# Clustered attention with two gated layers: another fetch offset in the planner, w_in in blocks of two half-height pieces with a common scale

## The chip, the cores and the metric

The kernel runs on one core of a Trainium2 chip. The metric is the device time of one execution in microseconds (us); lower is better. The engines are TensorE (PE, with its weight loads as PEld), VectorE (DVE), ScalarE (ACT), GpSimd (POOL) and SyncE (SP, whose queue issues every DMA here). The kernel before took 785.26 us (median of 3 runs, 783.64 to 786.57).

## The reference, cut to what matters

Inputs are q, k and v of 2 batches, 8 heads, 768 positions and 64 channels, 16 centroids for each head, and two weight pairs: w_in of 512x2048 and w_out of 2048x512, drawn as float64.

```python
q_assign = argmax(einsum(q_n, c_n)); k_assign = argmax(einsum(k_n, c_n))
mask   = q_assign[..., :, None] == k_assign[..., None, :]
scores = where(mask, scale * q @ k.T, -1e9)
attn   = exp(scores - max) / (sum + 1e-9)
x  = (attn @ v) as 1536 x 512                                  # both batches
h  = x @ w1_in;  x2  = (h * sigmoid(h)) @ w1_out               # layer 1
h  = x2 @ w2_in; out = (max(h,0) + alpha * min(h,0)) @ w2_out  # layer 2
```

## The kernel before

All operands of a matmul are split into a high and a low fp16 part under a power-of-two scale, so that a product takes three matmuls (high by high, high by low, low by high).

**Attention.** There are 12 query tiles of 128 rows and 8 heads, so 96 units. `front(u)` makes the scores of a unit in two PSUM banks (L793, L797), takes their bound on DVE (L807), the exponential on ACT (L812), the fp16 parts on ACT (L819) and DVE (L821); a DMA transpose (L827) turns them, and `back(u)` multiplies them with v (L839, 18 matmuls) two units later. When the eight heads of a tile are through, `x_done` scales the tile (L865), splits it on POOL (L868, L869) and transposes it (L870). Keys, values and queries are prepared by `prep_k_*`, `prep_v*` and `prep_q_*`, with transposes of their own (L638, L684, L730, L746).

**Weights.** A float64 weight piece arrives as pairs of 32-bit words in a raw buffer of 8 KB for each partition (`load_piece`, L893), 1 MB at a time. `to_f32` makes float32 of it: two ACT passes (L904, L908) and two DVE passes (L915, L918). Then the sum of squares is taken: for the first layer on PE (`sum_sq_pe`, L953, with a DVE reduction at L955), for the second on ACT (L945). For w_in, `scale(j)` sums over the partitions on PE (`all_sum`, L498), makes a power-of-two scale and its inverse (`pow2_scale`: L445 on DVE, L450 and L453 on POOL), splits the piece into its fp16 parts (`split`, mode "a": L930 on ACT, L931 on DVE) and then loads the next piece into the raw buffer that came free. w_in has 8 pieces, each of 256 columns and all 512 rows. The first layer has 4 raw buffers, the second 3, and each layer's w_out follows in the same buffers. w_out's 8 pieces share one scale: all are converted first (`conv`), `scale` sums over them, and only then are they split (`piece`, L930 and L931 again).

**Layers.** Layer 1 runs beside attention in 7 chunks of one or two tiles (`layer1`, L1187 for w1_in and L1218 for w1_out, with a tanh, three elementwise passes at L1194 to L1199 and an ACT copy at L1225). Layer 2 runs in 3 blocks of 512 rows: 16 column tiles through w2_in (L1289, 192 matmuls a block; L1298, L1299, L1302, L1303 on DVE and ACT), then 4 row tiles through w2_out (L1320, 192 matmuls). The second layer's raw buffers and the split parts of w2_in lie where the keys, values and queries of attention lay; those of w2_out where the first layer's weights lay.

**Order.** The program is written in Python in some order, and then `plan_order` fixes the order on every engine. `Plan` holds a cost for each instruction (`costs`), follows the data's dependences, and lays the program out in its own time, 61 times with some noise, forward and backward; the best layout's order is what the engines execute. Two parts of the model matter here. A DMA from DRAM costs a fixed part and its bytes by a rate that depends on the length of a contiguous run (L104 to L106). And PE's instructions are taken to be fetched in blocks of 256: a counter `fetched` starts at some value, is raised by 2 for each matmul (the weight load and the matmul), and when it passes 256 the DMAs in flight at that moment are made later by 0.4 or 1.1 us (L224, L277 to L289). The order is fixed, not the times: an engine waits in its place for whatever is late.

## Time and profile before

| | |
|---|---|
| median of 3 runs | 785.26 us |
| profiled execution | 784.7 us, span 782.8 us |
| PE busy | 679.5 us, 87% of the span |
| DVE, ACT, POOL busy | 541.3, 466.5, 136.2 us |
| DMA packets of the instruction queue | 52, 0.85 MB in all |
| w_in, w_out loads | 16 each, 1024 KB each |
| DMA transposes | 149 |

"Busy" is the time in which an engine executed; a share of the span is an average over stages that differ. The program has five: a start in which keys, queries and weights are prepared (to about 40 us), a stage in which the first layer's weights are converted beside the first units of attention (to 120 us), a short one in which layer 1 has begun but the weights are not all done (to 180 us), the long one with attention and layer 1 side by side (to 440 us), and the preparation of the second layer's weights beside the last of layer 1 (to 560 us). After that PE works through layer 2.

### The profile page before, as it was taken

How to read it: one execution, taken by the hardware profiler on the slowest of the kernel's cores; microseconds unless marked ns; L12 is line 12 of the kernel's file. 1: busy time of each engine (PE TensorE's matmuls, PEld its weight loads, DVE VectorE, ACT ScalarE, POOL GpSimd, SP SyncE). 2: the span in 40 equal slices, each digit the busy share in tenths (PEclk: the TensorE clock that was granted, in tenths of full speed). 3: DMA queues.
4: the chain of work that ended last, by engine and by line, in shares of the span. 5: the costliest groups of instructions: out<-in, count | busy, mean ns of one | idle time of the engine just before them, and what ended most of it. 6: DMA issues, size and time to landing. Idle time of an engine off the chain costs nothing.

```text
span 782.8 us, 16346 instructions
## 1 busy us (share of the span) xinstructions
PE 679.5 (87%) x6730; PEld 475.0 (61%) x6730; DVE 541.3 (69%) x992; ACT 466.5 (60%) x757; POOL 136.2 (17%) x237
## 2 busy tenths in 40 slices
PE   0254559679999999998999999888999999999998
PEld 0243448568887878887788898774444444444443
DVE  4689998898779578867876886878970385018700
ACT  6875976777778667756765898997640141012200
POOL 3562131123404732121130001000000000000000
PEclk9999978899999999999999999999999999999999
DMA  7989997989999996996898986452000000000000
GB/s 216 300 201 294 300 214 125 156 168 152 165 160 158 186 162 129 155 167 125 138 142 135 243 225 187 160 172 100 1 15 27 14 1 0 28 28 1 0 28 27
DMA packets 241593, 101.85 MB, mean 130 GB/s; under 512 B 217328, under 2 KB 227568, under 8 KB 241392
## 3 DMA queue, kind: packets, MB, share of 16 engines
q1 hardware_dynamic: 241520, 100.83, 60.4%
q8 instruction: 52, 0.85, 0.4%
q14 instruction: 21, 0.17, 0.1%
HBM read 44.08 MB, written 3.15 MB: 60 GB/s over the span
## 4 chain that ended last, share of the span: by engine, by line
PE 36%; ACT 7%; DMA 5%; DVE 2%; issue 1%; POOL 0%; SPq 0%; ACTq 0%
PE w L1320 11%; PE w L1289 10%; PE m L1320 5%; PE m L1289 5%; DMA arena<-in_moe_w_out_dram 2%; PE w L1218 2%; ACT arena L904 2%; ACT arena L908 2%; ACT arena L945 1%; PE w L1187 1%; DMA arena<-arena 1%; DMA arena<-in_moe_w_in_dram 1%; PE x L839 1%; PE s L793 1%; PE s L797 1%
## 5 line engine op out<-in xcount | busy, mean ns | idle before, releaser
L1218 PE MATMUL w<-arena 128*128 128x256 f16 (+1 forms) x1248 | 150.1, 258 | 3.7 <-ACT arena L1225 1.9
L1187 PE MATMUL w<-arena 128*128 128x256 f16 (+1 forms) x1200 | 142.0, 257 | 3.1 <-DVE arena L1195 1.7
L1218 PEld LDWEIGHTS <-arena 128*128 128x128 f16 x1344 | 113.2, 99 | 22.3 <-issue 5.7
L1187 PEld LDWEIGHTS <-arena 128*128 128x128 f16 x1344 | 111.9, 98 | 23.3 <-issue 8.3
L821 DVE TENSOR_TENSOR arena<-arena 128x768 f16<-128x768 f32 x96 | 96.8, 1009 | 30.4 <-ACT arena L819 30.0
L839 PE MATMUL x<-arena 128*128 128x64 f16 x1728 | 108.6, 198 | 10.1 <-DMA arena<-arena 8.0
L812 ACT ACTIVATE arena<-s,stat 128x768 f32<-128x768 f32 x96 | 85.9, 895 | 38.1 <-DVE s L807 18.4
L807 DVE TENSOR_SCALAR_CACHE_REDUCE s<-s,stat 128x768 f32<-128x768 f32 x96 | 97.6, 1019 | 12.2 <-PE s L797 10.4
L839 PEld LDWEIGHTS <-arena 128*128 128x128 f16 x1728 | 90.6, 102 | 21.2 <-DMA arena<-arena 10.9
L819 ACT ACTIVATE arena<-arena 128x768 f16<-128x768 f32 x96 | 80.3, 837 | 30.2 <-DMA arena<-arena 29.5
L1320 PEld LDWEIGHTS <-arena 128*128 128x128 f16 x576 | 56.4, 98 | 68.0
L1289 PEld LDWEIGHTS <-arena 128*128 128x128 f16 x576 | 55.7, 98 | 68.5 <-issue 2.4
L1289 PE MATMUL w<-arena 128*128 128x512 f16 x384 | 94.1, 379 | 0.0
L1320 PE MATMUL w<-arena 128*128 128x512 f16 x384 | 85.8, 379 | 0.0
L1298 DVE TENSOR_SCALAR arena<-w,stat 128x512 f32<-128x512 f32 x32 | 23.9, 747 | 78.8 <-PE w L1289 78.7
L793 PE MATMUL s<-arena 80*128 80x384 f16 x192 | 68.6, 357 | 9.9 <-ACT arena L812 9.7
L1302 ACT ACTIVATE arena<-arena,stat 128x512 f16<-128x512 f32 x48 | 34.4, 718 | 69.2 <-DVE arena L1299 69.2
L797 PE MATMUL s<-arena 128*128 128x384 f16 x192 | 68.5, 357 | 0.0
L450 POOL TENSOR_SCALAR stat<-stat 128x1 int32<-128x1 int32 x49 | 12.4, 256 | 290.1 <-DVE stat L445 197.1
L915 DVE SCALAR_TENSOR_TENSOR arena<-arena 128x1024 int32<-128x1024 int32 x32 | 41.3, 1290 | 22.2 <-ACT arena L908 22.1
L1289 PE MATMUL m<-arena 128*128 128x512 f16 x192 | 51.3, 379 | 0.1
L931 DVE SCALAR_TENSOR_TENSOR arena<-arena,stat 128x1024 f16<-128x1024 f32 x32 | 41.6, 1306 | 5.0 <-ACT arena L930 5.0
(145 smaller groups left out, 969.2 us busy)
## 6 DMA issues: line engine op xcount, KB each, us to landing
arena<-in_moe_w_in_dram SPq DMA_DIRECT2D x16, 1024.0 KB, 6.3
arena<-in_moe_w_out_dram SPq DMA_DIRECT2D x16, 1024.0 KB, 5.9
arena<-in_k_dram SPq DMA_DIRECT2D x8, 384.0 KB, 5.1
arena<-in_q_dram SPq DMA_DIRECT2D x6, 512.0 KB, 5.2
arena<-in_v_dram SPq DMA_DIRECT2D x8, 384.0 KB, 6.2
out_dram<-arena SPq DMA_DIRECT2D x12, 256.0 KB, 2.0
arena<-arena SPq DMA_TRANSPOSE x149, 4.0
arena<-in_moe_alpha_dram SPq DMA_DIRECT2D x1, 1024.0 KB, 5.3
```

Source lines behind the costliest of these rows:

```text
L793: nc.tensor.matmul(out=sc[:, j, :hs], lhsT=qt2[0:D + C, h], rhs=kt2[0:D + C, h % 2, j * hs:(j + 1) * hs], start=True, stop=False,)
L797: nc.tensor.matmul(out=sc[:, j, :hs], lhsT=qt1[:, h], rhs=kt1[:, h % 2, j * hs:(j + 1) * hs], start=False, stop=True,)
L807: nc.vector.tensor_scalar(sc[:, :, :hs], sc[:, :, :hs], nd_cols[:, H * (n % 2) + h:H * (n % 2) + h + 1], None, op0=ALU.mult, op1=ALU.min, ...
L812: nc.scalar.activation(out=view(o, F32, 2, hs), in_=sc[:, :, :hs], func=ACTF.Exp, scale=-1.0, bias=bias, accum_out=sums[n % 2][:, h:h + 1],)
L819: nc.scalar.activation(out=hl[:, 0], in_=p, func=ACTF.Copy)
L821: en.tensor_tensor(out=hl[:, 1], in0=p, in1=hl[:, 0], op=ALU.subtract)
L839: nc.tensor.matmul(out=x_ps[0][:, h], lhsT=pt[:, ph * T + t], rhs=vt[:, h % 2, t, vh], start=(i == 0), stop=(i == 3 * T - 1),)
L931: nc.vector.scalar_tensor_tensor(out=lo, in0=t, scalar=s, in1=hi, op0=ALU.mult, op1=ALU.subtract)
L1187: nc.tensor.matmul(out=hp[:, ff], lhsT=wi[:, a, kd, ff * 128:ff * 128 + 128], rhs=mov(bb, kd), start=(i == 0), stop=(i == 3 * KD - 1),)
L1218: nc.tensor.matmul(out=acc, lhsT=wo[:, a, f % 2, dt * 128:(dt + 1) * 128], rhs=g[:, f, bb], start=(i == 0), stop=(i == 3 * KF - 1),)
L1289: nc.tensor.matmul(out=hp, lhsT=in_piece(o_a + 24 * KB, f // 2)[:, a, kd, f % 2 * 128:][:, :128], rhs=x[bb][:, kd], start=(i == 0), stop=( ...
L1320: nc.tensor.matmul(out=acc, lhsT=g[:, f, a, t * 128:(t + 1) * 128], rhs=out_piece(o_w, f // 2)[:, bb, f % 2], start=(i == 0), stop=(i == 3 ...
```

## The change

Three things change. The planner's counter of PE instructions starts at 50 in place of 190, so a fetch is taken to come after 206 instructions, and then every 256, in place of after 66 and then every 256; and the planner's DMA rates are 395 for runs of 4 KB and more (400) and 350 for runs of 2 KB (290). A piece of w_in is 512 columns of 256 rows in place of 256 columns of 512 rows: the bytes of a piece are the same, its contiguous runs are 4 KB in place of 2 KB. Two pieces, the upper and the lower half of the same 512 columns, form a block with a common scale: there are four `scale` tasks for each w_in in place of eight; each waits for both pieces' sums, splits both, and only then loads the next two.

```diff
-        rate = 400.0 if run >= 4096 else 290.0 if run >= 2048 else 380.0
+        rate = 395.0 if run >= 4096 else 350.0 if run >= 2048 else 380.0
...
-        fetched, flight = 190, []
+        fetched, flight = 50, []
...
     def all_sum(cols, kind="m"):
-        n = cols[0].shape[1]
-        ps = psum(kind, n)
-        for i, c in enumerate(cols):
-            top = c.bitcast(BF16).rearrange("p (n t) -> p n t", t=2)[:, :, 1]
-            nc.tensor.matmul(out=ps, lhsT=ones, rhs=top, start=(i == 0), stop=(i == len(cols) - 1))
+        if not isinstance(cols[0], list):
+            cols = [cols]
+        n = cols[0][0].shape[1]
+        ps = psum(kind, n * len(cols))
+        for q, line in enumerate(cols):
+            for i, c in enumerate(line):
+                top = c.bitcast(BF16).rearrange("p (n t) -> p n t", t=2)[:, :, 1]
+                nc.tensor.matmul(
+                    out=ps[:, q * n:(q + 1) * n], lhsT=ones, rhs=top, start=(i == 0), stop=(i == len(line) - 1)
+                )
...
-    def in_piece(o, j):
-        return view(o + 4 * KB * j, F16, 2, KD, FW)
+    def in_block(o, f):
+        return view(o + 8 * KB * (f // 4), F16, 2, KD, 2 * FW)[:, :, :, f % 4 * 128:f % 4 * 128 + 128]
...
-                return load_piece(w[:, j * FW:(j + 1) * FW], raw(j))
+                n = w.shape[0] // 2
+                return load_piece(w[j % 2 * n:(j % 2 + 1) * n, j // 2 * 2 * FW:(j // 2 + 1) * 2 * FW], raw(j))
...
-        def scale(j):
+        def scale(b):
...
-            tot = all_sum([ss[:, j:j + 1]], kind)
-            pow2_scale(tot, 1, 15, None, m.s[:, j:j + 1], m.inv[:, j:j + 1])
-            d = in_piece(o_dst, j)
-            t = raw(j)[:, :, 1].bitcast(F32).rearrange("p (a f) -> p a f", a=KD)
-            split(t, d[:, 0], d[:, 1], m.s[:, j:j + 1], modes[j])
-            load(j + len(raws))
+            both = range(2 * b, 2 * b + 2)
+            tot = all_sum([[ss[:, j:j + 1] for j in both]] * 2, kind)
+            pow2_scale(tot, 2, 15, None, m.s[:, both[0]:both[0] + 2], m.inv[:, both[0]:both[0] + 2])
+            for j in both:
+                d = view(o_dst + 8 * KB * b, F16, 2, 2, PC)[:, :, j % 2]
+                t = raw(j)[:, :, 1].bitcast(F32)
+                split(t, d[:, 0], d[:, 1], m.s[:, j:j + 1], modes[j])
+            for j in both:
+                load(j + len(raws))
...
-            if j:
-                tasks.append(m.scales[j - 1])
+            if j and j % 2 == 0:
+                tasks.append(m.scales[j // 2 - 1])
```

The matmuls of both layers take the same weights from their new places (`in_block`), in the same number. Since the planner's costs change, the order changes on every engine.

The first place is DVE's queue just ahead of the first `x_done` (the last row of each fence, on which layer 1's first chunk depends). Before:

```order
L955 SCALAR_TENSOR_TENSOR arena,stat<-w_69,arena 128x128
L915 SCALAR_TENSOR_TENSOR arena<-arena 128x1024
L918 SCALAR_TENSOR_TENSOR arena<-arena 128x1024
L807 TENSOR_SCALAR s_65,stat<-s_65,stat 128x2x384
L915 SCALAR_TENSOR_TENSOR arena<-arena 128x1024
L955 SCALAR_TENSOR_TENSOR arena,stat<-w_68,arena 128x128
L821 TENSOR_TENSOR arena<-arena 128x768
L807 TENSOR_SCALAR s_64,stat<-s_64,stat 128x2x384
L918 SCALAR_TENSOR_TENSOR arena<-arena 128x1024
L865 TENSOR_TENSOR arena<-x,stat 128x512
```

And in the changed kernel, whose lines lie 5 further down (L920 is L915, L923 is L918, L960 is L955, L812 is L807, L826 is L821, L870 is L865):

```order
L812 TENSOR_SCALAR s_64,stat<-s_64,stat 128x2x384
L1186 TENSOR_SCALAR stat<-stat 128x1 x3
L920 SCALAR_TENSOR_TENSOR arena<-arena 128x1024
L923 SCALAR_TENSOR_TENSOR arena<-arena 128x1024
L812 TENSOR_SCALAR s_65,stat<-s_65,stat 128x2x384
L826 TENSOR_TENSOR arena<-arena 128x768
L960 SCALAR_TENSOR_TENSOR arena,stat<-w_68,arena 128x128
L920 SCALAR_TENSOR_TENSOR arena<-arena 128x1024
L826 TENSOR_TENSOR arena<-arena 128x768
L870 TENSOR_TENSOR arena<-x,stat 128x512
```

Over the whole queue up to that row, the changed kernel has one L807 less, one L821 more, one L918 less, two L955 less and four L445 less; everything else ahead of it is the same in number.

The second place is SP's queue from the load of alpha on (the second layer's weights; a number behind an x repeats the row). Before:

```order
L1242 DMA arena<-in_moe_alpha_dram 128x2048
L893 DMA arena<-in_moe_w_in_dram 128x4x512
L827 DMA_TRANSPOSE arena<-arena 128x12x128 x2
L893 DMA arena<-in_moe_w_in_dram 128x4x512 x2
L827 DMA_TRANSPOSE arena<-arena 128x12x128 x2
L893 DMA arena<-in_moe_w_in_dram 128x4x512
L870 DMA_TRANSPOSE arena<-arena 128x8x128
L893 DMA arena<-in_moe_w_in_dram 128x4x512 x3
L893 DMA arena<-in_moe_w_out_dram 128x2x1024 x8
```

And now (L898 is L893, L832 is L827, L875 is L870):

```order
L1251 DMA arena<-in_moe_alpha_dram 128x2048
L898 DMA arena<-in_moe_w_in_dram 128x2x1024
L832 DMA_TRANSPOSE arena<-arena 128x12x128
L898 DMA arena<-in_moe_w_in_dram 128x2x1024
L832 DMA_TRANSPOSE arena<-arena 128x12x128 x2
L898 DMA arena<-in_moe_w_in_dram 128x2x1024 x2
L875 DMA_TRANSPOSE arena<-arena 128x8x128
L898 DMA arena<-in_moe_w_in_dram 128x2x1024 x3
L898 DMA arena<-in_moe_w_out_dram 128x2x1024 x8
```

Pieces 3 and 4 are now issued together behind the last two transposes of attention; before, piece 3 went with piece 2, ahead of them.

The third place is ACT's queue at the end of the second layer's weights: the last conversions of w_out (L904, L908, L945) among the 16 passes of layer 2's first block (L1302), up to the first split of w_out (L930). Before:

```order
L908 ACTIVATE arena<-arena 128x1024
L1302 ACTIVATE arena<-arena,stat 128x512
L904 ACTIVATE arena<-arena 128x1024
L908 ACTIVATE arena<-arena 128x1024
L945 ACTIVATE arena,stat<-arena 128x1024
L1302 ACTIVATE arena<-arena,stat 128x512
L1266 ACTIVATE arena,stat<-arena 128x512 x3
L1302 ACTIVATE arena<-arena,stat 128x512
L1266 ACTIVATE arena,stat<-arena 128x512
L945 ACTIVATE arena,stat<-arena 128x1024
L1302 ACTIVATE arena<-arena,stat 128x512 x3
L930 ACTIVATE arena<-arena,stat 128x1024
```

And now (L909 is L904, L913 is L908, L950 is L945, L1311 is L1302, L1275 is L1266, L935 is L930):

```order
L950 ACTIVATE arena,stat<-arena 128x1024
L909 ACTIVATE arena<-arena 128x1024
L913 ACTIVATE arena<-arena 128x1024
L1311 ACTIVATE arena<-arena,stat 128x512 x2
L909 ACTIVATE arena<-arena 128x1024
L913 ACTIVATE arena<-arena 128x1024
L950 ACTIVATE arena,stat<-arena 128x1024
L1311 ACTIVATE arena<-arena,stat 128x512
L1275 ACTIVATE arena,stat<-arena 128x512 x4
L950 ACTIVATE arena,stat<-arena 128x1024
L1311 ACTIVATE arena<-arena,stat 128x512 x2
L935 ACTIVATE arena<-arena,stat 128x1024
```

The first split stood behind 6 of the 16 passes of layer 2's first block, the last behind 9; now they stand behind 10 and 14. On PE, the last of the eight partial sums of the second layer's w_out stood behind 66 of the first block's 192 matmuls at L1289, and now behind 132.

## Rows read from the trace of the kernel before

**Rows 1.** Busy time by stage: stretch, its length, PE, PEld, DVE, ACT, POOL, clock, DMA, GB/s.

```profile
0.00:40.00 40.00, 7.19 (x101) 5.65 (x101) 22.31 (x67) 30.81 (x49) 19.98 (x51) 1.00 0.93 261
40.00:120.00 80.00, 45.90 (x483) 33.34 (x480) 75.90 (x155) 59.91 (x79) 26.48 (x37) 0.93 0.99 248
120.00:180.00 60.00, 47.11 (x763) 39.43 (x762) 53.01 (x103) 44.93 (x83) 15.26 (x23) 0.90 0.83 151
180.00:440.00 260.00, 249.37 (x3411) 213.10 (x3408) 200.73 (x401) 181.98 (x331) 68.71 (x101) 0.99 0.91 152
440.00:560.00 120.00, 110.96 (x968) 84.31 (x966) 99.00 (x135) 105.70 (x152) 5.12 (x22) 1.00 0.55 164
```

**Rows 2.** Timeline of DVE and PE: start, us, engine, line; the first x_done, layer 1's start.

```profile
109.85 0.68 DVE L865 TENSOR_TENSOR arena<-x,stat 128x512 f32<-128x512 f32 x1
...
121.83 0.44 PE L1187 MATMUL w<-arena 128*128 128x128 f16 x4
```

**Rows 3.** Groups of DVE by line and shape: busy us, mean ns of one.

```profile
L807 DVE TENSOR_SCALAR_CACHE_REDUCE s<-s,stat 128x768 f32<-128x768 f32 x96 | 97.6, 1019 | 12.2 <-PE s L797 10.4 <-ACT arena L819 1.5 <-ACT arena L1225 0.3
L821 DVE TENSOR_TENSOR arena<-arena 128x768 f16<-128x768 f32 x96 | 96.8, 1009 | 30.4 <-ACT arena L819 30.0
...
L918 DVE SCALAR_TENSOR_TENSOR arena<-arena 128x1024 int32<-128x1024 int32 x32 | 38.9, 1218 | 0.2
...
L955 DVE SCALAR_TENSOR_TENSOR arena<-w,arena 128x128 bf16<-128x128 f32 x16 | 4.5, 282 | 0.9 <-PE s L498 0.4 <-PE w L953 0.3
...
L445 DVE TENSOR_SCALAR stat<-s 128x1 int32<-128x1 int32 x21 | 3.0, 151 | 7.6 <-PE s L498 7.6
```

**Rows 4.** PE's waits from 120 to 440 us: us in total, times, longest.

```profile
PE x L839 <- DMA arena<-arena: 8.0, 8, 2.2
```

**Rows 5.** DMA in 149.4:149.8, then 413.4:414.2, then 246.3:247: queue; issues, us to landing.

```profile
q8 instruction: 1, 0.02, 22.9%
...
arena<-arena SPq DMA_TRANSPOSE x1, 5.8
...
arena<-arena SPq DMA_TRANSPOSE x1, 3.7
```

**Rows 6.** Busy time and instruction counts (x) up to two fetches of instructions.

```profile
0.00:149.58 149.58, 76.65 (x987) 59.08 (x987) 122.19 (x280) 111.55 (x170) 53.48 (x99) 0.95 0.94 230
...
0.00:413.82 413.82, 324.34 (x4434) 270.37 (x4435) 333.07 (x692) 300.53 (x509) 128.66 (x209) 0.97 0.92 182
```

**Rows 7.** One w_in load alone; eight w_out loads; landing of that w_in load.

```profile
484.00:491.00 7.00, 6.76 (x64) 5.90 (x62) 6.50 (x8) 7.00 (x11) 0.00 (x0) 1.00 0.48 150
497.00:537.00 40.00, 35.27 (x282) 26.57 (x280) 30.32 (x38) 34.12 (x48) 0.68 (x4) 1.00 0.60 211
...
arena<-in_moe_w_in_dram SPq DMA_DIRECT2D x1, 1024.0 KB, 5.1
```

**Rows 8.** Second layer's weights: timeline, the chain's DMAs, waits from 440 to 545.

```profile
452.12 3.58 SPq L893 DMA_DIRECT2D arena<-in_moe_w_in_dram  x2
...
463.19 1.22 ACT L930 ACTIVATE arena<-arena,stat 128x1024 f16<-128x1024 f32 x1
...
498.33 7.30 DMA arena<-in_moe_w_out_dram
513.24 6.13 DMA arena<-in_moe_w_out_dram
529.99 5.96 DMA arena<-in_moe_w_out_dram
...
ACT arena L904 <- DMA arena<-in_moe_w_out_dram: 5.7, 5, 2.0
PE s L498 <- ACT arena L945: 4.8, 6, 2.1
...
531.55 4.04 PE L1289 MATMUL w<-arena 128*128 128x512 f16 x18
...
571.49 3.83 PE L1320 MATMUL w<-arena 128*128 128x512 f16 x17
```

More of the change, by code (lines that the diff above doesn't have):

```diff
@@ L979, in conv @@
                 sum_sq_pe(view(raws[j % len(raws)], BF16, PC, 4)[:, :, 3], ss[:, j:j + 1], kind)
-        def scale(j):
+        def scale(b):
             if not w2:
-                for o in range(4 * j, 4 * j + 4):
+                for o in range(8 * b, 8 * b + 8):
                     assert o < 8 or (("k", 0, (o - 8) // 3) if o < 20 else ("v", 0, (o - 20) // 3)) in did
-            tot = all_sum([ss[:, j:j + 1]], kind)
-            pow2_scale(tot, 1, 15, None, m.s[:, j:j + 1], m.inv[:, j:j + 1])
-            d = in_piece(o_dst, j)
-            t = raw(j)[:, :, 1].bitcast(F32).rearrange("p (a f) -> p a f", a=KD)
-            split(t, d[:, 0], d[:, 1], m.s[:, j:j + 1], modes[j])
-            load(j + len(raws))
-            if j == NPC - 1:
+            both = range(2 * b, 2 * b + 2)
[7 more added lines that the diff above has]
+                load(j + len(raws))
+            if b == NPC // 2 - 1:
                 nc.vector.tensor_reduce(out=m.smin, in_=m.s, axis=AX.X, op=ALU.min)
@@ L995, in in_tasks @@
         m.loads = [lambda j=j: load(j) for j in range(len(raws))]
-        m.scales = [lambda j=j: scale(j) for j in range(NPC)]
+        m.scales = [lambda b=b: scale(b) for b in range(NPC // 2)]
         for j in range(NPC + 1):
@@ L1174, in layer1 @@
             j = f // 2
-            wi = in_piece(o_w, j)
+            wi = [in_block(o_w, f // 2 * 2 + ff) for ff in range(2)]
             if c == 0 and f % 2 == 0:
@@ L1187, in layer1 @@
                             nc.tensor.matmul(
-                                out=hp[:, ff], lhsT=wi[:, a, kd, ff * 128:ff * 128 + 128],
+                                out=hp[:, ff], lhsT=wi[ff][:, a, kd],
                                 rhs=mov(bb, kd), start=(i == 0), stop=(i == 3 * KD - 1),
@@ L1289, in layer2 @@
                     nc.tensor.matmul(
-                        out=hp, lhsT=in_piece(o_a + 24 * KB, f // 2)[:, a, kd, f % 2 * 128:][:, :128],
+                        out=hp, lhsT=in_block(o_a + 24 * KB, f)[:, a, kd],
                         rhs=x[bb][:, kd],
@@ L1368, in cluster_attention_silu_prelu @@
             if c == 0:
-                while i < KF and w1["in"].scales[i // 2] in bg:
+                while i < KF and w1["in"].scales[i // 4] in bg:
                     run_bg(1)
```

## The prediction

> **What bounds the kernel now.** I read the busy time by stage first, then PE's waits and the chain of waits inside the stages in which PE is idle, and last the groups of instructions for prices. By stage [rows 1], PE is idle 32.8 of the first 40 us, 34.1 of the next 80, 12.9 of the next 60, 10.6 of the 260 us in which attention and layer 1 run side by side, and 9.0 of the 120 us in which the second layer's weights are prepared. From 560 us on it is busy to the end. So the time is PE's own work and what it idles in the first 180 us and between 440 and 560 us, with a remainder in the long stage. In the stage from 40 to 120 us it is DVE that is full: 75.9 of 80 us, with DMA at 0.99. The first x_done stands at 109.85 us on DVE and layer 1 begins on PE at 121.83 us [rows 2]; until then PE has only attention's units. Between 440 and 560 us ACT is busy 105.7 and DVE 99.0 of 120 us, and the chain that ended last runs through the second layer's weights: a load, its conversion, the next load into the same buffer [rows 8].
>
> **Term A, the start.** The new order puts less work on DVE ahead of the first x_done: one L807 less (1.02 us), one L821 more (1.01), one L918 less (1.22), two L955 less (0.56) and four L445 less (0.60) [rows 3], together 2.4 us. As DVE has 4.1 us of idle time in those 80 us [rows 1], layer 1 should begin about 2.4 us earlier, and PE, which waits for it, gains that. The pairing itself should cost nothing here: with four buffers two pieces are in hand while two others load. The bounds are wider, since the order of the first 40 us also decides: DVE's idle time there is 17.7 us [rows 1], a part of which could go, and a first pair that waits for its second load would add at most one load's landing, 5.1 us [rows 7]. I take -2.4, with -6 and +5 as ends.
>
> **Term B, the fetches of instructions.** While attention and layer 1 run side by side PE waits 8 times for a transposed unit, 8.0 us in all [rows 4]. In six of these eight, with 6.6 us of the eight, the queue that brings instructions has a packet of 16 KB in the 4 us ahead of the wait; the longest, 2.2 us, follows the fetch in the window at 149.4 us [rows 5]. A transpose in flight at a fetch landed 5.8 us after its issue, one without a fetch 3.7 us [rows 5]. So a fetch makes a transpose late by up to 2 us, and the order is planned around the places where the planner believes the fetches to be. Up to the fetch at 149.58 us PE and its weight loads had begun 987 + 987 = 1974 instructions, up to the one at 413.82 us 4434 + 4435 = 8869 [rows 6]: 182 and 165 beyond a multiple of 256. The counter before expects a fetch 66 beyond a multiple, 99 to 116 instructions from there; the new one expects it at 206, 24 to 41 from there. So the new plan has its slack nearly where the fetches are. Of the 6.6 us I take 5 as gone; the ends are 0 (the late transposes only meet other waits) and -8.0, all of the row.
>
> The Trainium skill, page "Runtime: NRT & Kernel Launch", section "Instruction fetch mechanics", speaks against this term: crossing a 16 KiB block of instructions costs one step of a DMA queue and is mostly hidden. For PE's own stream the trace does not contradict that; for transposes in flight the two landings above do. By the page the term would be 0, as in the first rival.
>
> **Term C, the second layer's weights.** Here the change adds a wait. Before, the load of piece 3 goes out with that of piece 2, within 3.6 us of 452.12 us, because piece 0 alone frees a buffer [rows 8]. Now piece 1 must be split too, whose ACT pass begins at 463.19 us and takes 1.22 [rows 8], with some 1.3 us on DVE behind it: pieces 3 and 4 load at about 466 us, 10 us later. What is queued behind these loads on SP is only later weights; for them ACT waits in its order, with layer 1's passes behind it. With three buffers and pairs, one piece can be converted ahead and every block costs a full round. A round of load and conversion took 513.24 - 498.33 = 14.9 and 529.99 - 513.24 = 16.8 us in w_out [rows 8]; a pair adds some 3 us of splits. Three blocks of 15 to 20 us put the last split of w_in at 511 to 526 us. w_out then needs three rounds less a part of one, as its first load finds the buffer of piece 5 free: 37 to 42 us, so that its last conversion ends at 548 to 568 us. The new order allows for much of it: on PE the last partial sum stands behind 132 of the block's 192 matmuls in place of 66. At 4.04 us for 18 matmuls, or 0.216 us from one to the next, and with the block ending at 571.49 us [rows 8], that place is at 571.5 - 60 x 0.216 = 558.5 us. The middle of the range, 558, meets it; the late end costs 9.5 us. The other way, fewer sums (four blocks in place of eight pieces) could take away the 4.8 us for which PE waits on them now [rows 8]. I take +2, with -4.8 and +9.5 as ends.
>
> **Small terms.** The block sums add 16 matmuls of one column on PE and take away 8 passes on DVE (0.15 us each [rows 3]) and 16 on POOL, which waits most of the time; I take 0. A w_in piece in runs of 2 KB takes 0.48 x 7 = 3.4 us of the DMA engines and one of w_out in runs of 4 KB 0.60 x 40 / 8 = 3.0 us [rows 7]. So 0.4 us a load are saved, 3 us of DMA time over the first layer's eight pieces, beside a DVE that is full; I take 0 there too. The planner, though, now reckons with about a microsecond less for each of these loads. That makes its plan tighter than the chip, and this is why term C is not taken below zero.
>
> The Trainium skill, page "Perfetto Trace Analysis", section "DMA Optimizations", says that going from 2 KB to 4 KB or 8 KB can raise throughput dramatically. The trace shows 3.4 against 3.0 us, an eighth. By the page the start would shorten more, as in the last rival.
>
> **The sum.** -2.4 - 5 + 2 = -5.4 us. From the profiled execution, 784.7 us (span 782.8 and 1.9 around it), that gives 779.3; the median of the runs stands 0.6 above that execution, so 780 us.
>
> **The rivals.**
>
> 1. The fetch offset buys nothing: the transposes are late all the same, and A and C cancel: 784.7 - 2.4 + 2, or about 785 with the 0.6. For it: the 8.0 us are 3% of that stage, and the planner already had random slack in it. Against it: six of eight waits follow a fetch.
> 2. Slower: the wait for pairs on three buffers decides. If block and w_out rounds run at the long end, the last sum of w_out comes at 568 us, PE stands in its order, and the splits of w_out come one by one as layer 2's second product asks for them: +9.5 us from C and nothing from B, 784.7 - 2.4 + 9.5 + 0.6, about 792 us. It decides from the point at which the last partial sum is later than 558.5 us plus what A and B gain. For it: in this stage ACT waits 5.7 us for w_out's loads and PE 4.8 us for sums already [rows 8]. Against it: the new order has moved that sum back by 66 matmuls, 14 us.
> 3. The loads in longer runs land so much sooner that the start shrinks by half of DVE's idle time in the first 40 us [rows 1], 8.8 us in place of A's 2.4; with B at 5 and C at 2 that is 784.7 - 8.8 - 5 + 2 + 0.6, about 774 us. For it: DMA is at 0.93 and 0.99 in the first two stages [rows 1]. Against it: 3.4 and 3.0 us a load [rows 7].
>
> **How the numbers follow.** The forecast has a chance of 0.50, with a range of its own from 775 to 783; rival 1 has 0.25, rival 2 0.17, rival 3 0.08. About 0.5% (3.9 us) is what a measurement of this kernel can tell from no change. Of the forecast's 0.50, 0.42 lie under 781.3; with rival 3 that makes 0.50 for faster. The rest of the forecast and most of rival 1 and a little of rival 2 make 0.31 for the same; slower has 0.19. The range that leaves out one in ten on each side is 772 to 791.
>
> **What would show it.** A: layer 1's first matmul on PE at about 119 us in place of 121.8. B: PE's waits for transposes between 120 and 440 us at 3 us in place of 8.0, and the idle time of the 120 to 440 us stages down by about 5. C: PE's idle time between 440 and 560 us at 9 to 13 us, ACT waiting for w_in's loads more than now, and the last partial sum of w_out near 558 us. The forecast is wrong if layer 1 begins later than now, if waits for transposes stay at 8, or if layer 2's second product begins with a wait.

## The result, and the profile after

The changed kernel takes 774.1 us (median of 4 runs, 773.3 to 776.8) against 784.45 of before: a ratio of 0.9865, 95% interval 0.9834 to 0.9896. The forecast was 780 with a range of 772 to 791. The profiled execution is at 773.9 us, its span 772.1 in place of 782.8. By stage, with the columns of [rows 1]:

```profile
0.00:40.00 40.00, 9.41 (x115) 6.59 (x115) 26.96 (x73) 33.53 (x53) 22.15 (x53) 1.00 0.97 286
40.00:120.00 80.00, 47.68 (x534) 35.23 (x535) 74.83 (x153) 59.34 (x81) 19.74 (x28) 0.66 1.05 244
120.00:180.00 60.00, 50.10 (x895) 43.00 (x893) 54.38 (x111) 48.75 (x92) 18.56 (x28) 1.00 0.89 164
180.00:440.00 260.00, 250.39 (x3369) 212.94 (x3367) 202.73 (x400) 183.60 (x330) 64.07 (x95) 1.00 0.92 158
440.00:560.00 120.00, 109.60 (x875) 78.07 (x874) 96.10 (x126) 98.19 (x141) 4.26 (x14) 1.00 0.44 139
```

PE idles 30.6 us in the first 40 (32.8 before) and DVE is busy 4.65 us longer there (26.96 against 22.31); PE's clock from 120 to 180 us is 1.00 in place of 0.90. The first x_done and layer 1's start, as in [rows 2]:

```profile
104.67 0.68 DVE L870 TENSOR_TENSOR arena<-x,stat 128x512 f32<-128x512 f32 x1
...
115.51 0.61 PE L1196 MATMUL w<-arena 128*128 128x128 f16 x4 [0.83 <-DMA arena<-arena]
```

Both come 5.2 and 6.3 us earlier. PE's and ACT's waits for transposes, 120 to 440 us, the first as in [rows 4] (us in total, times, longest):

```profile
PE x L844 <- DMA arena<-arena: 8.9, 12, 1.6
...
ACT arena L824 <- DMA arena<-arena: 19.7, 20, 2.5
```

and ACT's in the kernel before:

```profile
ACT arena L819 <- DMA arena<-arena: 29.5, 25, 3.4
```

PE waits no less than before (8.9 against 8.0 us); ACT, which writes the operand that a transpose reads and must wait until it is through, waits 9.8 us less. The second layer's weights, as in [rows 8], first by time, then by waits (440 to 560 us):

```profile
454.20 2.70 SPq L898 DMA_DIRECT2D arena<-in_moe_w_in_dram  x2
...
471.88 2.44 SPq L898 DMA_DIRECT2D arena<-in_moe_w_in_dram  x2
...
547.78 0.16 PE L501 MATMUL s<-stat,arena 128*128 128x1 bf16 x1 [1.78 <-ACT arena L950]
...
560.42 0.38 PE L1329 MATMUL w<-arena 128*128 128x512 f16 x1
```

```profile
PE s L501 <- ACT arena L950: 5.7, 6, 1.8
...
ACT arena L909 <- DMA arena<-in_moe_w_in_dram: 6.7, 5, 2.4
```

and ACT's wait for w_in before, in the same 120 us:

```profile
ACT arena L904 <- DMA arena<-in_moe_w_in_dram: 2.4, 2, 1.6
```

Pairs of loads stand 17.7 us apart; ACT waits 6.7 us for w_in where it waited 2.4; the last partial sum of w_out comes at 547.8 us, after PE has waited 1.8 us for ACT, and layer 2's second product follows its first without a wait.

To compare orders that differ, PE's work is cut at places that every kernel has: I to layer 1's first matmul, II to the last matmul of its 8th group of w_out (48 matmuls each), III to the last of its 48th group of w_in (24 each), IV to layer 2's second product, V to the end. The lengths, in us, are each from one profiled execution, which stood up to 3.3 us from the median of its kernel's runs (3: +3.3, 11: +3.2, 8: -3.1), so a difference of 2 or 3 us in one stretch says little alone. "near" says whether the planner's fetches stand within about 40 instructions of where the real ones mostly are: [rows 6] has two of them, 182 and 165 beyond a multiple of 256, and half of the 52 in that trace lie between 166 and 213. The ratio is to runs of before on the same chip.

| kernel | near | median, us | ratio, 95% interval | I | II | III | IV | V |
|---|---|---|---|---|---|---|---|---|
| before | no | 784.45 | | 121.8 | 96.1 | 236.0 | 117.6 | 211.3 |
| after | yes | 774.10 | 0.9865, 0.9834 to 0.9896 | 115.5 | 89.1 | 236.0 | 119.8 | 211.7 |
| 1 counter and rates | yes | 776.34 | 0.9874, 0.9827 to 0.9922 | 119.1 | 96.1 | 234.0 | 111.8 | 212.1 |
| 2 pieces alone | no | 780.85 | 0.9937, 0.9911 to 0.9964 | 120.9 | 91.5 | 236.5 | 118.6 | 211.4 |
| 3 before, other noise | no | 784.14 | 0.9978, 0.9952 to 1.0005 | 120.9 | 97.2 | 237.2 | 118.9 | 211.5 |
| 4 after, shifted | no | 779.01 | 0.9909, 0.9874 to 0.9944 | 117.3 | 91.1 | 234.3 | 121.6 | 211.7 |
| 5 counter alone | yes | 771.02 | 0.9806, 0.9776 to 0.9837 | 118.4 | 95.3 | 230.9 | 112.5 | 212.3 |
| 6 rates alone | no | 781.68 | 0.9951, 0.9926 to 0.9976 | 116.3 | 96.8 | 237.0 | 117.1 | 211.7 |
| 7 pieces and counter | yes | 774.44 | 0.9854, 0.9823 to 0.9884 | 119.4 | 91.8 | 231.5 | 118.6 | 211.5 |
| 8 pieces and rates | no | 776.73 | 0.9875, 0.9840 to 0.9909 | 116.0 | 96.7 | 230.7 | 116.0 | 211.7 |
| 9 counter alone, shifted | no | 776.59 | 0.9895, 0.9869 to 0.9921 | 118.8 | 98.8 | 229.2 | 114.7 | 212.3 |
| 10 before, shifted | yes | 775.01 | 0.9872, 0.9846 to 0.9898 | 122.1 | 94.7 | 229.0 | 114.0 | 211.3 |
| 11 pairs in layer 1 only | yes | 775.56 | 0.9877, 0.9850 to 0.9903 | 118.5 | 99.3 | 234.9 | 112.7 | 211.7 |
| 12 counter, other noise | yes | 775.01 | 0.9853, 0.9811 to 0.9895 | 117.1 | 95.2 | 235.1 | 113.8 | 211.9 |

So the change gained 6.3 us in I and 7.0 in II, nothing in III, and gave back 2.2 in IV and 0.4 in V.

### The profile page after: what moved, and what is told of

Its sections match the earlier page's. It is cut to its first block, busy times and chain, and to the rows that moved or that the text cites. A ratio compares the mean times of both kernels' runs of the same rounds, so it can differ in the third digit from the quotient of the medians.

```text
span 772.1 us, 16335 instructions
## 1 busy us (share of the span) xinstructions
PE 675.5 (87%) x6746; PEld 470.1 (61%) x6746; DVE 539.4 (70%) x984; ACT 464.8 (60%) x757; POOL 129.5 (17%) x221
## 4 chain that ended last, share of the span: by engine, by line
PE 43%; DMA 9%; ACT 8%; DVE 2%; issue 1%; POOL 1%; SPq 0%; ACTq 0%; DVEq 0%
PE w L1329 11%; PE w L1298 8%; PE m L1329 5%; PE w L1196 5%; PE m L1298 4%; PE w L1227 4%; DMA arena<-arena 3%; DMA arena<-in_moe_w_out_dram 3%; DMA arena<-in_moe_w_in_dram 3%; PE x L844 2%; ACT arena L913 1%; ACT arena L909 1%; ACT arena L950 1%; PE s L798 1%; PE s L802 1%
## 5 line engine op out<-in xcount | busy, mean ns | idle before, releaser
L1227 PEld LDWEIGHTS <-arena 128*128 128x128 f16 x1344 | 110.4, 98 | 23.0 <-DVE arena L936 5.4
L1196 PEld LDWEIGHTS <-arena 128*128 128x128 f16 x1344 | 112.4, 98 | 19.4 <-issue 3.1
L844 PE MATMUL x<-arena 128*128 128x64 f16 x1728 | 102.7, 197 | 16.4 <-DMA arena<-arena 16.3
L826 DVE TENSOR_TENSOR arena<-arena 128x768 f16<-128x768 f32 x96 | 95.0, 991 | 26.4 <-ACT arena L824 25.7
L812 DVE TENSOR_SCALAR_CACHE_REDUCE s<-s,stat 128x768 f32<-128x768 f32 x96 | 98.0, 1021 | 17.6 <-PE s L802 16.7
L844 PEld LDWEIGHTS <-arena 128*128 128x128 f16 x1728 | 85.4, 100 | 29.3 <-DMA arena<-arena 21.6
L1298 PEld LDWEIGHTS <-arena 128*128 128x128 f16 x576 | 55.8, 98 | 71.6 <-issue 6.4
L1329 PEld LDWEIGHTS <-arena 128*128 128x128 f16 x576 | 56.3, 98 | 68.0 <-DVE arena L1312 0.2
L1311 ACT ACTIVATE arena<-arena,stat 128x512 f16<-128x512 f32 x48 | 34.1, 720 | 67.7 <-DVE arena L1308 67.7
L450 POOL TENSOR_SCALAR stat<-stat 128x1 int32<-128x1 int32 (+1 forms) x41 | 12.3, 303 | 303.4 <-DVE stat L445 226.0
L920 DVE SCALAR_TENSOR_TENSOR arena<-arena 128x1024 int32<-128x1024 int32 x32 | 39.2, 1224 | 24.0 <-ACT arena L913 24.0
L909 ACT ACTIVATE arena<-arena 128x1024 int32<-128x1024 uint32 x32 | 36.7, 1147 | 23.0 <-DMA arena<-in_moe_w_out_dram 13.1
```

The source lines that it names most:

```text
L812: nc.vector.tensor_scalar(sc[:, :, :hs], sc[:, :, :hs], nd_cols[:, H * (n % 2) + h:H * (n % 2) + h + 1], None, op0=ALU.mult, op1=ALU.min, ...
L826: en.tensor_tensor(out=hl[:, 1], in0=p, in1=hl[:, 0], op=ALU.subtract)
L844: nc.tensor.matmul(out=x_ps[0][:, h], lhsT=pt[:, ph * T + t], rhs=vt[:, h % 2, t, vh], start=(i == 0), stop=(i == 3 * T - 1),)
L909: nc.scalar.activation(out=lo, in_=lo.bitcast(U32), func=ACTF.Copy, scale=0.87475 * 2.0 ** -29, bias=0.49)
L1196: nc.tensor.matmul(out=hp[:, ff], lhsT=wi[ff][:, a, kd], rhs=mov(bb, kd), start=(i == 0), stop=(i == 3 * KD - 1),)
L1227: nc.tensor.matmul(out=acc, lhsT=wo[:, a, f % 2, dt * 128:(dt + 1) * 128], rhs=g[:, f, bb], start=(i == 0), stop=(i == 3 * KF - 1),)
```

## The experiments

Three theories. **Theory 1**, the forecast's: the order gains because the planner's fetches stand where the real ones come. **Theory 2**: the gain belongs to something else that the change names, the pieces and pairs or the rates (each expectation says which). **Theory 3**: any new order moves the time by a few us, up or down, whatever the numbers in the planner mean; such an order is called a draw below.

### One part at a time (1, 2, 5 to 8)

The three parts (counter, rates, pieces) make eight kernels; before and after are two of them, these are the other six. The rates are changed in 1, 6 and 8, the counter in 1, 5 and 7:

```diff
-        rate = 400.0 if run >= 4096 else 290.0 if run >= 2048 else 380.0
+        rate = 395.0 if run >= 4096 else 350.0 if run >= 2048 else 380.0
...
-        fetched, flight = 190, []
+        fetched, flight = 50, []
```

2, 7 and 8 have the changed kernel's pieces, scales and layers 1 and 2.

1, counter and rates:

> The kernel before with the planner's part of the change alone: the counter starts at 50 and the rates are 395 and 350; pieces, loads and scales as before. Theory 1 (the prediction's term B: a fetch offset near the real one lets the order cover the late transposes): about 5 us faster than before, 779, with PE's waits for attention's transposes between 120 and 440 us at 3 us in place of 8. Theory 2 (the gain belongs to the pieces and pairs, which bring the first layer's weights sooner): 784 to 786, first L1187 near 121.8 us as before. Theory 3 (any new order moves the time by several us, up or down, whatever the numbers mean): anything from 776 to 792, the waits for transposes still near 8 us, and the difference from before sitting in the first 200 us.

2, pieces alone:

> The changed kernel with the planner's numbers of before (190, 400 and 290): half-height pieces of 512 columns and pairs with a common scale alone. Theory 1: the prediction's terms A and C alone, -2.4 + 2, so 784 us. Theory 2: the whole gain, 773 to 776 us, first matmul of layer 1 near 115.5 us and the 16th split of w_out on DVE near 159 us, as in the changed kernel. Theory 3: anything from 770 to 792 us, with a start that is neither that of before nor that of after.

5, counter alone:

> The kernel before with the counter at 50 alone. The first experiments gave 776.3 for the planner's two numbers together, 780.9 for the pieces alone, and no weight to the real place of the fetches (waits for transposes 7.6 us with the planner's numbers, 6.5 with everything half a block away). Theory 1 (the counter): about 776 to 778, a wait for transposes well below 8 us. Theory 2 (the rates: a planner that takes w_in's loads for faster orders the weights' conversion tighter): 784 to 786, as before. Theory 3 (every redraw of the order is a draw of a few us): between 776 and 788, and this run and the next don't add up to the -9.1 us of both together.

6, rates alone:

> The kernel before with the rates 395 and 350 alone, the counter at 190. Theory 1: 784 to 786. Theory 2: about 776 to 778, with layer 1's fourth chunk of w_out sums and the second layer's blocks about 5 us earlier between 450 and 530 us, as with both numbers. Theory 3: 776 to 788, no sum with the run before.

7, pieces and counter:

> The changed kernel with the rates of before (400 and 290), the counter at 50. Only w_in's price of a load in the planner changes little here, since its runs are 4 KB now and 400 against 395 is all that differs for them; other DMAs with runs of 2 KB keep 290. Theory 1: as after, 773 to 776. Theory 2: as the pieces alone, 780 to 782. Theory 3: 771 to 784, with the difference from after in the first 200 us.

8, pieces and rates:

> The changed kernel with the counter of before (190), the rates 395 and 350. Theory 1: as the pieces alone, 780 to 782. Theory 2: as after, 773 to 776. Theory 3: 771 to 784, and neither this run nor the one before lies where after lies for a reason that the other shares.

Measured against the median of before in their own runs, in us: 1 -9.1, 2 -4.6, 5 -14.6, 6 -3.9, 7 -11.2, 8 -8.9, and after -10.4. The counter is worth -14.6 alone, -5.2 on top of the rates, -6.6 on top of the pieces and -1.5 on top of both: below zero each time, -7.0 in the mean, though the -1.5 is within the noise of the two medians. The pieces are worth -4.6 alone, -5.0 with the rates, but +3.4 and -1.3 with the counter; the rates -3.9, +5.5, -4.3 and +0.8. So neither of these two has a worth of its own that the runs can name, and the sizes don't add up, as theory 3 has it; the counter's sign is theory 1's. Theory 1's own figures were met in 7 alone: 2, 6 and 8, whose counter is unchanged, came out 2 to 4 us below them (780.9 for 784, 781.7 for 784 to 786, 776.7 for 780 to 782), and so did 1 and 5 (776.3 for 779, 771.0 for 776 to 778). The forecast's sign of it, PE's waits for attention's transposes, failed: they are 7.6, 6.9 and 5.3 us in 1, 5 and 7, and 2.9 in 6, whose counter is unchanged. In 5 most of the gain, 10.2 of the 14.4 us between the two profiled executions, is in III and IV (columns as above):

```profile
213.70:444.60 230.90, 225.16 (x2898) 191.19 (x2896) 180.40 (x352) 163.01 (x289) 57.96 (x85) 0.99 0.91 160
444.60:557.20 112.60, 107.96 (x864) 77.47 (x863) 97.05 (x131) 98.72 (x144) 5.11 (x20) 1.00 0.46 142
```

### The same order, the fetches elsewhere (4, 9, 10)

A draw of the order can't explain a kernel whose order stays. 64 matmuls that the planner does not see stand ahead of all others on PE. The order of all other instructions on every engine stays word for word, and what follows stands 128 instructions, half a block, later against the fetches. They go into the changed kernel (4), the counter alone (9) and the kernel before (10); lines lie 10 further down (7 at L498).

```diff
-    plan = Plan(list(nc.cur_bb.bb.instructions))
+    plan = Plan([i for i in nc.cur_bb.bb.instructions if i.name not in shift])
...
         nc.vector.memset(ones, 1.0)
+        for _ in range(64):
+            shift.append(nc.tensor.matmul(out=bank_w[0][:, :32], lhsT=ones, rhs=ones[:, :32], start=True, stop=True).ins.name)
```

> The changed kernel with 64 small matmuls of 32 columns ahead of PE's first work, which the planner does not see: every engine keeps its order of after word for word, but all that follows on PE stands 128 instructions later against the blocks of 256, half a block. They run while PE has nothing to do (it is idle for most of the first 40 us); at most 4 us of them could show. Theory 1: the planner's fetches are now half a block from the real ones, the late transposes come back: 4 to 8 us slower than after, PE's waits for transposes between 120 and 440 us up from 8.9 to 13 us or more. Theories 2 and 3: the place of the fetches is of no weight; within 1.5 us of after, the waits for transposes within 2 us of 8.9.

> The counter-only kernel (771.0 us) with the 64 small matmuls ahead of PE's work that the planner doesn't see: its order is kept word for word, the real fetches stand half a block from where the planner has them. Theory 1 (the counter gains because it stands near the real fetches): most of the 14.5 us is lost, 778 to 786 us, above all in the two stretches where it was gained, layer 1 from its 8th group of w_out matmuls to its 48th of w_in (230.9 us, to go back to 235 or 236) and from there to layer 2's second product (112.5 us, to go back to 116 or 118). Theory 3 (the counter only made another order, which happens to be a good one): 770 to 774 us, the two stretches within 1.5 us.

> The kernel before (order word for word) with the same 64 matmuls: its counter, which expects a fetch at 66 beyond a multiple of 256, now stands near the real ones, which come at about 40 to 55 in its own count. Theory 1: 5 to 10 us faster than before with no change of the order at all, 775 to 780, the stretch to the 48th group of w_in down from 236 to 232 or so. Theory 3: within 2 us of before, at most the 1.9 us of the small matmuls slower.

The added group, in experiment 4 (0 to 40 us), costs PE 1.9 us of time that it idles:

```profile
L548 PE MATMUL w<-arena 128*128 128x32 bf16 x64 | 1.9, 188 | 1.1 <-DVE arena L546 1.1
```

Experiment 10 is theory 1's: the order of before with its fetches moved to where its planner had them is 11.0 us faster, which no theory of orders gives. 4 and 9 move the fetches away from a plan that had them. 4 is 4.9 us slower than after by the medians, and 3.9 when each is set against before on its own chip; every run of 4 lies above every run of after, but the intervals of the two ratios overlap, and the expected waits didn't come (6.5 us where after has 8.9). 9 is 5.6 us slower than the counter alone (776.59 against 771.02, and 5.2 against before on their own chips, with intervals apart), a little under what was expected; the loss is in II and IV, and III, where it was expected, is 1.7 us shorter. The 64 matmuls themselves aren't the cause, as the same ones make two kernels slower and one faster. Before, and then 10, by stretch:

```profile
0.00:121.80 121.80, 54.87 (x597) 40.49 (x598) 100.01 (x226) 92.39 (x130) 46.76 (x88) 0.94 0.96 250
121.80:217.90 96.10, 82.05 (x1414) 71.07 (x1412) 80.64 (x162) 72.14 (x139) 28.05 (x40) 0.95 0.92 157
217.90:453.90 236.00, 226.24 (x2900) 191.88 (x2899) 182.93 (x355) 164.08 (x287) 55.95 (x85) 0.99 0.90 158
453.90:571.50 117.60, 108.88 (x864) 77.61 (x863) 98.88 (x132) 98.79 (x145) 4.78 (x20) 1.00 0.42 135
```

```profile
0.00:122.10 122.10, 59.10 (x661) 43.70 (x662) 99.94 (x226) 92.06 (x130) 46.76 (x88) 0.76 0.96 249
122.10:216.90 94.80, 81.70 (x1414) 70.24 (x1413) 80.77 (x162) 72.59 (x139) 27.87 (x40) 0.96 0.93 159
216.90:445.90 229.00, 223.92 (x2901) 191.03 (x2899) 182.43 (x357) 164.68 (x288) 56.72 (x85) 1.00 0.95 163
445.90:559.90 114.00, 108.82 (x863) 77.58 (x861) 97.63 (x130) 98.23 (x144) 4.77 (x20) 1.00 0.44 139
```

The work is the same. In III PE's idle time falls from 9.8 to 5.1 us and its busy time by 2.3, with a granted clock of 1.00 in place of 0.99; in IV the idle time falls from 8.7 to 5.2.

As the order is the same, the 149 transposes of the two traces can be set side by side, one by one. A transpose is counted as met by a fetch if a packet of queue 8 began between 0.5 us ahead of its issue and its landing. 51 were met only in before: they landed a median 4.84 us after their issue there and 3.72 in experiment 10. 50 were met only in 10: 3.74 and 4.67. The 32 met in neither took 3.75 and 3.76. So a fetch makes a transpose about 1 us late, whichever transpose it is. The number that it meets stays (67 and 66), so what differs is which. The 32 loads of weights, counted in the same way, show the like in this pair: 13 were met only in before (a median 6.63 us, and 5.70 in 10), 8 only in 10 (5.68, and 6.60).

Here is one transpose that counts, in before: the fetch (DMA in 374.2:374.3), the landing of the transpose issued at 370.85 us (in 370.8:370.9), and what waits behind it (queue; us to landing; then the timeline, with the idle time ahead and what ended it in brackets).

```profile
q8 instruction: 1, 0.02, 64.8%
...
arena<-arena SPq DMA_TRANSPOSE x1, 5.5
```

```profile
376.41 0.84 ACT L819 ACTIVATE arena<-arena 128x768 f16<-128x768 f32 x1 [2.32 <-DMA arena<-arena]
...
377.29 0.96 DVE L821 TENSOR_TENSOR arena<-arena 128x768 f16<-128x768 f32 x1 [1.96 <-ACT arena L819]
...
379.48 0.19 PE L839 MATMUL x<-arena 128*128 128x64 f16 x1 [1.61 <-DVE arena L865]
```

And the same transpose (in 363.6:363.7), the same ACT and DVE passes and the same matmul in experiment 10, with no fetch in its flight:

```profile
arena<-arena SPq DMA_TRANSPOSE x1, 4.3
```

```profile
368.02 0.84 ACT L829 ACTIVATE arena<-arena 128x768 f16<-128x768 f32 x1 [1.13 <-DMA arena<-arena]
...
368.90 0.96 DVE L831 TENSOR_TENSOR arena<-arena 128x768 f16<-128x768 f32 x1 [0.76 <-ACT arena L829]
...
371.09 0.19 PE L849 MATMUL x<-arena 128*128 128x64 f16 x1 [0.42 <-DVE arena L875]
```

The late transpose holds the buffer that ACT writes next; ACT holds DVE, whose pass L865 stands behind in its order, and PE loses 1.61 us to "DVE L865", where it loses 0.42 in 10. In the words of the profile's page this is no wait for a DMA, and the row by which the prediction measured the fetches doesn't contain it.

### Other noise (3, 12)

```diff
-        noise = Random(1)
+        noise = Random(2)
```

3 is before with it, 12 the counter alone with it.

> The kernel before with another seed (2 in place of 1) for the planner's noise: the same work, the same model, another order. Theories 1 and 2: within 2 us of before, 783 to 787, since a planner that lays the program out 61 times and keeps the best should end at about the same place. Theory 3: away from before by 3 us or more, either way, and mostly in the first 200 us.

> The kernel before with the counter at 50 and the other seed (2) for the planner's noise: the pair of the third experiment (784.1 us with that seed and the counter at 190). Theory 1 (the counter, by where it puts the fetches; the fixed orders of the fourth, ninth and tenth experiments speak for it): 770 to 777 us, at least 7 us below that pair, the stretch from layer 1's 8th group of w_out to its 48th of w_in at 230 to 234 us (237.2 in the pair) and the next at 112 to 115 (118.9). Theory 3 (771.0 was a lucky order): 778 to 786, within 5 us of the pair.

Another order of before takes the same time (784.1, interval up to 1.0005), though PE's waits for transposes (120 to 440 us) nearly double:

```profile
PE x L839 <- DMA arena<-arena: 15.6, 18, 1.9
```

With the counter at 50 it is at 775.0: a second pair in which the counter is worth -9.6 us (against their own runs of before). Theory 1's total holds; of its places, IV does (113.8), III misses by 1 us (235.1). Against the counter alone with the first seed it is 4.0 us slower by the medians (3.7 against their own runs of before, with intervals that overlap): an order may draw about that much.

### What the runs seemed to point to (11)

Pairs for the first layer, single pieces for the second (`in_single` is the kernel before's `in_tasks`), the counter at 50, the rates of before.

```diff
-        w2["in"] = in_tasks(w2_in, raws, o_a + 24 * KB, "s", SPLIT[2], EXP_ON[2])
+        w2["in"] = in_single(w2_in, raws, o_a + 24 * KB, "s", SPLIT[2], EXP_ON[2])
...
-                        out=hp, lhsT=in_block(o_a + 24 * KB, f)[:, a, kd],
+                        out=hp, lhsT=in_piece(o_a + 24 * KB, f // 2)[:, a, kd, f % 2 * 128:][:, :128],
```

> A version put together from what the runs point to: counter at 50, rates of before, half-height pieces and pairs for the first layer's w_in alone, single pieces of 256 columns for the second layer's. With the first layer's pairs the stretch from layer 1's first matmul to its 8th group of w_out took 89 to 92 us (96 without) in three of four kernels, and with single pieces and the counter at 50 the stretch of the second layer's weights 112 us (118.6 to 119.8 with pairs). If both hold in one order (theory 2, the pieces act stage by stage): 765 to 768 us, faster than after and than the counter alone. If the numbers are draws (theory 3): 768 to 778, with one of the two stretches not where it was.

It isn't better: 775.6. IV is as hoped (112.7); II is the longest of all (99.3), as theory 3 allows, though in an execution that was the slowest of the kernel's six.

The fastest version run is the counter alone, 771.0 us; its interval (0.9776 to 0.9837) meets that of after (0.9834 to 0.9896) only at the edge.

Over all: the seven kernels with the fetches near their places stand 9.1 to 14.6 us below before, 11.1 in the mean; the seven without 0 to 9.4, 4.9 in the mean. The two ranges overlap by a little (9 has 9.4, 1 has 9.1). The stretch that follows the counter most steadily is IV: with single pieces in the second layer it is 111.8 to 114.0 us in the five kernels with the fetches near (1, 5, 10, 11, 12) and 114.7 to 118.9 in the four without (before, 3, 6, 9). III doesn't (229.0 to 236.0 and 229.2 to 237.2).

## Why the prediction came out as it did

The direction was right, and so was one mechanism, the largest term's. The gain of 10.4 us is twice the forecast's 5.4, and it doesn't sit where the forecast put it. 774.1 us lies just below the forecast's own 775 to 783 and on rival 3's 774. That is luck, as rival 3 has 8.8 us at the start, 5 in the waits for transposes and nothing in stretch II, and none of the three measured so.

**Term A** (-2.4, ends -6 and +5) measured -6.3 in stretch I, outside its ends: it is the mis-sized term. The step that failed is that the first x_done would move by the 2.4 us of work that DVE no longer has ahead of it, its idle time staying as it was. Busy time up to the first x_done, with the columns of [rows 1] (DVE is the third engine), before and then after:

```profile
0.00:109.85 109.85, 46.38 (x511) 34.17 (x512) 88.06 (x204) 85.14 (x119) 44.03 (x85) 0.99 1.00 263
```

```profile
0.00:104.67 104.67, 45.00 (x511) 32.51 (x512) 87.07 (x195) 81.99 (x116) 38.89 (x77) 0.79 1.00 262
```

DVE's busy time falls by 1.0 us only, as some of the passes that stay take longer. Its idle time falls by 4.2 us (21.8 to 17.6), by 4.65 in the first 40. Together that is the 5.2 us by which the x_done comes earlier; the last 1.1 lies between it and layer 1. The prediction named that idle time and kept it as a bound only; that it would shrink is rival 3's mechanism. Rival 3's cause, that loads in longer runs land sooner after their issue, isn't seen. The eight loads of the first layer's w_in, 0 to 62 us, before and then after (count, KB, median us to landing):

```profile
arena<-in_moe_w_in_dram SPq DMA_DIRECT2D x8, 1024.0 KB, 7.3
```

```profile
arena<-in_moe_w_in_dram SPq DMA_DIRECT2D x8, 1024.0 KB, 7.4
```

The Trainium skill, page "Perfetto Trace Analysis", section "DMA Optimizations", says that going from transfers of 2 KB to 4 KB can raise throughput dramatically; these landings don't bear it out. Nor do the pieces make the start by themselves: with the old planner (2) I is 120.9 us. The table points to the rates, and the prediction gave them nothing: I is 116.3, 116.0 and 115.5 us with them (6, 8, after) and 121.8, 120.9 and 119.4 in the same kernels without (before, 2, 7). But it is 119.1 with them in 1 and 118.4 without in 5, so what shortened the start stays open.

**Stretch II** (-7.0) the prediction did not have. In the changed kernel it reads:

```profile
115.50:204.60 89.10, 78.06 (x1376) 68.41 (x1377) 76.97 (x157) 69.59 (x135) 23.62 (x35) 0.98 0.94 163
```

Beside the second row of before above, PE idles 11.0 in place of 14.0 us and is busy 4.0 us less: the granted clock, a mean of its two levels of 2.4 and 1.2 GHz, is 0.98 in place of 0.95 (by an estimate, 0.02 of 89.1 and 0.05 of 96.1 us, 3 us apart), and 38 recorded matmuls fewer lie in it. The part of the clock need not be the change's, as the executions of before alone had mean clocks from 0.948 to 0.993. PE's waits for transposed units, the row of term B, in II and then in III, before:

```profile
PE x L839 <- DMA arena<-arena: 7.3, 7, 2.2
...
PE x L839 <- DMA arena<-arena: 0.6, 1, 0.6
```

And after:

```profile
PE x L844 <- DMA arena<-arena: 2.9, 6, 1.0
...
PE x L844 <- DMA arena<-arena: 5.9, 6, 1.6
```

So that row moved from II to III and did not go. Four of the five kernels with pairs in both layers have 89 to 92 us in II and one 96.7, while 11, with pairs in layer 1, has 99.3. So the pairs often help there, but what makes the stretch short is not settled.

**Term B** (-5). Right in its cause: experiments 5, 10 and 12, and 9 the other way, with 4 as a weaker sign. Wrong in the step from the cause to a row: "Of the 6.6 us I take 5 as gone" counted only the waits of PE for a transposed unit. Those are 8.9 us after, so that one of the prediction's own signs of being wrong came true, and III is 236.0 as before. The evidence for that row was weaker than it looked: 33 fetches fall in those 320 us, one every 9.7 us, so a moment has one in the 4 us ahead of it in four cases of ten by chance; and a fetch makes a transpose about 1 us late, not 2. By experiment 10 the fetches cost before 11.0 us, of which that row shows 1.2 (8.0 to 6.8): the rest stands under other names, as in the example, and in stretch IV. The row in experiment 10, 120 to 440 us:

```profile
PE x L849 <- DMA arena<-arena: 6.8, 7, 1.9
```

In the changed kernel ACT's waits for transposes fell by 9.8 us, but not by the counter: they are as low in 2, whose counter is unchanged (first row), and in 4, whose fetches are moved away (16.7 us), but not in 5 (second row).

```profile
ACT arena L824 <- DMA arena<-arena: 18.5, 24, 2.6
```

```profile
ACT arena L819 <- DMA arena<-arena: 27.4, 27, 3.3
```

Which part of the 10.4 us the counter brought there is open: by 7 and 2 it is 6.6, by after and 8 it is 1.5, by 4 it is 3.9 to 4.9.

The Trainium skill, page "Runtime: NRT & Kernel Launch", section "Instruction fetch mechanics", calls crossing a block mostly hidden. No run here contradicts that for PE's own stream; it says nothing of a DMA in flight, and there experiment 10 decides against rival 1, by which the fetch offset buys nothing.

**Term C** (+2, ends -4.8 and +9.5) came out at +2.2, and that the sizes agree is luck, as it is two effects: by the single runs the counter takes 5.1 us off IV (5 against before), which the prediction did not have there, and pairs put 6.1 on it where the counter is at 50 (7 against 5). The pair's late loads and ACT's wait for w_in are as foreseen. The last sum came at 547.8 us, 107 us into stretch IV; the forecast's 558 stands 104 us into it in before, which begins 13.3 us later. Rival 2 needed that sum later than its place in PE's order, and it was, but by 1.8 us; PE's waits for these sums are 5.7 us in place of 4.8, far from the 9.5 of that rival.

**Small terms.** The rates, taken as a tighter plan, moved the time by -4.3 to +5.5 us: no effect of their own on the whole is shown.

## What to carry to other kernels

A cost that strikes whatever is in flight at fixed places of a program is best measured by moving the places with the order kept, not by one row of waits: the late DMA reaches the bounding engine under the names of other engines. And when a planner makes a new order, a difference of about 4 us of 780 between two orders needs a second order before it is put down to the edit.

## What the runs showed of the hardware

A fetch of PE's instructions (one packet of 16 KB on queue 8) makes a DMA transpose in flight about 1 us late (3.72 to 4.84 and 3.74 to 4.67 us on the same transposes), and in the same two traces a load of weights by 0.9 (5.70 to 6.63 and 5.68 to 6.60); in the other two pairs with the same order (after and 4, 5 and 9) a transpose is late by 0.8 to 1.1 us and a load of weights by 0.1 to 0.9. Half a block's shift of the fetches was worth 11.0 us of 786 in an unchanged order.

PE's clock before layer 1 seems to cost little in this kernel: in stretch I it was granted a mean of 0.94 in before and 0.76 in experiment 10 (whose fetches stand elsewhere, too), and the stretch took 121.8 and 122.1 us, while PE was busy only 54.9 and 59.1 us of it. The executions of one kernel agree: of the 20 of before beside experiments 1 to 4, the 8 with a granted clock of 0.978 or more, a mean over the whole span, took a median 784.76 us, and the 12 with 0.963 or less 785.95.
